# A new order for all engines, and two halves of the last output block kept apart, in a fused attention and state-space kernel

## The chip, the cores and the metric

The kernel runs on one core of a Trainium2 chip. Its engines are TensorE (PE, matmuls, which write PSUM), VectorE (DVE), ScalarE (ACT), GpSimd (POOL) and the queue of SyncE (SP), from which nearly all transfers are issued. PSUM has eight banks, each of which holds one 128 x 512 float32 tile. The metric is the device time of one execution in microseconds (us). Each engine works through its own instructions in the order in which the program gives them, and semaphores make it wait for the others.

## The reference

Two blocks without a common input, their outputs side by side, for 2048 tokens of width 448:

```python
# A: sliding, dilated attention; 16 heads of 28; 8 keys at distances 0, 2, .. 14
qkv = x @ wqkv                        # (2048, 1344)
logits[h, s, w] = q[h, s] . k[h, s - 2 * w] * 28 ** -0.5   # masked where s - 2w < 0
a = (softmax(logits) . v, heads joined) @ wo
# B: a diagonal state-space layer with a complex state of 448
Bu = x @ B_bar.T
h[t] = Lam_bar * h[t - 1] + Bu[t]
y = 2 * Re(h @ C.T) + x * Dskip
out = concatenate([a, y], -1)         # (1, 2048, 896) bfloat16
```

## The kernel before

The program is a set of small steps and one long text, `ORDER`, that names 559 of them in the order in which they are emitted. A step such as `QK021@67` is the function `QK` with the digits as arguments, and `@67` names the PSUM banks that it takes. A dot behind an eviction means that ACT does it, an equals sign DVE. Every engine, and the SP queue, gets its own steps in the order of that text, so the text sets all orders at once. A step that takes a bank waits until the step that evicts the bank's last tile is done.

The steps that matter here, with their lines:

- Set-up (L139 to L222, ahead of `ORDER`): loads of x and of the weights on SP, and `wq6`, a packed copy of the last 64 columns of q and k, which POOL makes (L222) when those columns have landed.
- `XI`, `XA`, `XH`: transposes of x on PE; `xi`, `xa`, `xh` evict them into `xT`. `WV4` is four matmuls on zeros that nothing reads.
- `QK u m k` (L332, matmuls at L242): the projections q and k for half u of the tokens and column block m, into two banks. With k = 0 it is three matmuls of 128 rows for each of two token halves s; with k = 1 the last 64 rows, the two halves side by side in the array. Whichever of the two comes first starts the sum. Column block m = 6 takes its weights from `wq6`. `QS` is the same for one s alone. `qk u m s` and `qh u s a` evict. `V_` and `v` do the same for v.
- `P u r ws` (L367): DVE multiplies q with four shifted copies of k, 128 x 2048; 28 of them. `E_ u r` (L379) sums them over the head with PE. `lt`, `TR`, `tr` turn the logits; `sma`, `smb`, `smc` are the softmax of one half u on DVE, ACT, DVE.
- `AL g`, `al`, `ad g`, `sp g` (L448 to L475): the weights of four token tiles are put into a band: PE shifts them, `al` evicts them into `Ak`, `ad` writes that to DRAM (`pd`), and the four transfers of `sp` read it back skewed into four slots of `PT`, which `pm` (POOL, L842) has zeroed. `PT` has 12 slots for 16 tiles, so `sp3` writes the slots of `sp0` again, and must wait until the AV steps of B = 0 have read them. `pm0`, `pm1`, `pm2` zero the slots of `sp0`, `sp1`, `sp2`; `pm3` zeroes `wo`, `pm4` the last two `Ak`. `OP` opens these late buffers in the place of the early ones, among them `Cn`, which the transposes `CD` read.
- `AV B hg par` (L495): attention output of half B; B = 0 needs `sp0` and `sp1`, B = 1 needs `sp2` and `sp3`. `av` evicts, `W_ b par` (L516) multiplies with `wo`, `w` evicts into one of six `ya` buffers, `ow` stores it.
- `LC`, `ci`, `CD`, `ca`, `cs`: the weights C, loaded, put together, transposed by DMA into `Cw`, and scaled.
- `BU g jp k`, `BR`, `z` (L680 to L697): B block, state group g, the inputs of four neighbouring tokens and their rotation; `UP`, `y` go up one level, `sa`, `sb`, `sd` scan pairs of groups on DVE, `DN`, `dn`, `H_`, `h` go back down.
- `C j ct`, `c`, `oc` (L774 to L789): the output block for token j of four and token tile ct: seven matmuls, an addition of x * Dskip (`xd` makes it) into one of eight buffers in `xnA`, a store. The block (2, 3) is done as two halves of 224 columns, `CH i`, `ch i`, `oh i`.

Of the kernel before, what the change touches and what calls it, by code (L numbers as in the profile page):

```python
# [11 lines left out]
ALU = mybir.AluOpType  # L12
ACTF = mybir.ActivationFunctionType

S, D, H, DH, W = 2048, 448, 16, 28, 8
# [6 lines left out]
HS = 4  # L22
# [7 lines left out]


ORDER = """
WU@0 XI0@1567 XI1 PP@2 xi0= xi1. xi2= xi3. WV4 QS00@3 pcopy pa pb QS10@4 qk000. pd_ pc XH1@5 pe XA10@6 xh1. XA11@7 ty0 xa10=
QK021@01 ty5 QK031@23 qk010. xa11= QS11@5 tf0 pf QS01@6 tf5 QK041@74 P000 QK020 qk001. ts05 ts00 pg QK040 ts15 ts10
ts20 qk021. QK030 qk041. rb2 ts25 qk011. QK050@61 qk030. P001 qk040. QK051 qk020. rb3 V_011@45 QK061@27 qk031. V_010
ty1 P010 ty2 qk051. QK060 qk050. tf1 v010. P011 V_100@03 ts01 v011. qh011. P020 V_001@16 V_101 V_111@45 V_000 v101.
P021 ts11 ts21 V_110 qh001. tf2 v100. qh000. P030 QK100@30 v000. hc0 qh010. rb0 QK110@21 v111. v001. ty4 E_00@7
v110. tf4 E_01@5 ts02 E_02 ts12 P031 ts04 QK101 QK111 V_401@64 V_400 qk111. P040 qk110. ts22 QK130@12 qk101= qk100.
v401. P041 BD v400. QK131 ts14 QK141@30 P050 QK161@46 ts24 QK140 ty3 qk130. P051 qk131. QK160 ty6 P060 E_03 qh100.
tf3 E_04 qk140. E_05 xt3 qk141. P061 V_500@12 qh101. qh110. tf6 qh111. E_06 ts03 V_501 P100 QK151@30 xt0 ts13  # L40
QK121@46 hc1 QK150 lt00 P101 v501. lt01 QK120 P110 ts06 xt1 v500. P111 TR0@7 qk120. E_10@2 qk150. V_511@14 P120
tr0. V_510 xt2 qk121. P121 V_410@37 qk151. ts16 v511. sma0 E_11@5 ts23 E_12 v510. V_411 v411. P130 v410. LC BU401@60
ts26 BU201@41 smb0 BU301@73 P131 BU300 P140 BU200 OZ z30. P141 XR BU400 z20. P150 BR31 BR21 z40. BU000@74 P151 z31.
ci0. P160 E_13 ci3. E_14 CD0 E_15 P161 ci2. BU001 BU311@63 BU310 z21. smc0 CD3 z00. ci1. BR41 BR32 CD2 E_16 z32.
BU210@17 lt10 lt11 CD1 z41. TR1@6 rb1 BU500@25 tr1. BR33 sma1 BR01 BU101@06 z33. z01. BU211 BU501 BU100 z50. xd1 OP
pm3 smb1 BR22 pm0 UP3 wo BU010@42 z22. smc1 z10. y3. BU011 ca3 BU111@10 AL0@3 BR02 BR11 al0. BR51 BU110 z11. ad0 pm1
z02. xd2 z51. BR12 AL1@3 z12. BR23 BR03 al1= ca6 BU601@64 BU511@51 xd3 BR13 ad1 BU510 z03. sp0 cs3 z13. z23. pm4 cs6
UP1 BR52 UP0 y1. UP2 xd0 BU600 y0. ca1 sa0 sp1 AL2@3 pm2 BU410@02 z52. z60. y2. sb0 ca4 BR61 BU411 BU611@56 BR42 sd0
BR53 BU610 al2. z61. ad2 z42. BR62 cs1 z53. DN0@7 DN1@3 z62. AL3@4 dn0 UP5 dn1 BR43 al3. H_20@0 sa2 BR63 z43. H_10@5
ad3 H_11@7 z63. UP4 y5. H_01@3 UP6 y4. H_21@4 sp2 H_00@1 y6. AV030@2 h10 ca2 AV010@6 h20 AV011@5 h11 av030. AV031@0  # L50
cs4 av010. AV000@7 av031. h01 AV020@2 av000. sb2 AV021@6 av020. AV001@0 av011. W_10@3 h21 ca5 sp3 sd2 W_30@7 av021.
W_20@2 av001. sa4 W_00@5 w20. DN2@4 DN3@6 ow20 w00. W_21@0 w30. ow00 dn2 W_11@2 w10. dn3 ow30 w21. sb4 W_31@5 ow10
ow21 H_13@7 H_22@4 w31. h00 H_02@3 H_23@6 ow31 H_03@0 w11. cs2 W_01@5 h02 ow11 ca0 H_12@1 AV131@2 h23 cs5 AV130@3
w01. sd4 AV101@6 av130. ow01 AV111@5 av131. AV100@3 av101. sa6 av111. AV121@2 av100. AV110@6 av121. h13 AV120@5
av110= DN4@3 W_71@2 av120. sb6 DN5@7 dn4 W_61@6 w71. sd6 W_41@5 ow71 w61. dn5 W_40@3 h03 w41. W_70@2 ow41 w40= ow61
h22 H_05@6 H_24@7 w70. ow40 W_60@5 h12 ow70 h24 DN6@0 H_15@3 W_51@4 cs0 W_50@2 h15 w51. w60. dn6 H_14@1 ow51 C32@7
w50= ow60 h14 H_04@4 C33@3 c32 h05 h04 H_26@0 H_25@5 c33 H_16@2 C31@1 h16 oc33 h26 oc32 C30@7 c31 oc31 C12@6 c30 h25
oc30 C10@4 c12 oc12 H_06@3 C21@2 h06 c10 C00@0 c21 oc10 oc21 C13@1 c00 oc00 C20@7 ow50 C02@5 C22@6 C01@3 c22 c20
oc22 c13 C11@4 oc20 c02 oc13 oc02 C03@2 c11 c01 oc11 CH0@0 oc01 c03 CH1@6 ch0 oc03 oh0 ch1 oh1
"""  # L60

@with_exitstack
def kernel(
# [17 lines left out]
    V = nc.vector  # L81
# [3 lines left out]
    SP = nc.sync  # L85
# [26 lines left out]
    def evict(e, o, i):  # L112
        (ACT.copy if e == "A" else V.tensor_copy)(o, i)  # L113
# [5 lines left out]
    xnA = xbuf.rearrange("p (t d) -> p t d", d=D)  # L119
# [39 lines left out]
    xnB = keep.tile([128, 4, T, D], BF16, tag="xnB")  # L159
# [65 lines left out]
    Ak0 = smp.tile([128, 2, 2560], BF16, tag="Ak0")  # L225
    V.memset(Ak0.rearrange("p k n -> p (k n)").bitcast(F32), 0.0)
    pds = [dram.tile([128, 2560], BF16, tag=f"pd{g}", name=f"pd{g}") for g in range(4)]
# [5 lines left out]
    pp = {}  # L233
# [214 lines left out]
    def AL(g):  # L448
# [5 lines left out]
        for w in range(W):  # L454
            cc = 32 * (3 - w // 2) + 16 * (w % 2)
            PE.matmul(p4[:, :, :, w, :], shf[:, 135 + w:263 + w], at(4 * g, 4, cc), start=(w == 0), stop=True, skip_group_check=True)  # L456
            if w > 0:
                n = 4 if g < 3 else 2
                PE.matmul(p4[:, 0:n, :, w, :], shf[:, 7 + w:135 + w], at(4 * g + 2, n, cc), start=False, stop=True,
                          skip_group_check=True)  # L460

    @op
    def al(g, e):
        evict(e, late["Ak"][g].rearrange("p (s n) -> p s n", n=40 * HS)[:, :, 0:W * HS],
              pp.pop(("al", g)).rearrange("p (s n) -> p s n", n=W * HS))

    @op
    def ad(g):
        SP.dma_start(pds[g][:], late["Ak"][g])

    @op
    def sp(g):
# [298 lines left out]
    out_b = out[0].rearrange("(q p h j) n -> j h q p n", q=2, p=128, h=2)  # L771
# [30 lines left out]
    @op  # L802
    def ch(i):
        j, ct = LAST
        if i == 0:
            pp["yo"] = xnA[:, late["m"] % 8]
            late["m"] += 1
        sl = slice(D // 2 * i, D // 2 * (i + 1))
        V.tensor_tensor(pp["yo"][:, sl], pp.pop(("ch", i))[:, 0:D // 2], xnB[:, ct, j, sl], ALU.add)

    @op
    def oh(i):
        j, ct = LAST
        SP.dma_start(out_b[j, ct // 2, ct % 2, :, D + D // 2 * i:D + D // 2 * (i + 1)], pp["yo"][:, D // 2 * i:D // 2 * (i + 1)])


    late = {}
# [39 lines left out]
    for step in ORDER.split():  # L857
        name, args, bank, e = re.fullmatch(r"([A-Za-z]+_?)(\d*)@?(\d*)([.=]?)", step).groups()
# [33 lines left out]
```

## Time and profile before

| | us |
|---|---|
| median of 3 runs | 135.94 (135.54 to 136.13) |
| the profiled execution | 135.48 |
| its span on the core | 133.3 |
| PE busy | 126.3 |
| DVE busy | 113.0 |
| ACT busy | 92.0 |
| POOL busy | 19.7 |

The span runs from the first to the last instruction of the program; the execution has 2.2 us more around it. A PE that is busy in the profile has a matmul in the pipeline; the time from one start to the next tells how long the array is taken. In the timeline and the chain of waits the columns are the start in us, the length in us, the engine, the line, what is written and read, and the count; in brackets stands how long the engine was idle before, and what ended that.

### The profile page before, as it was taken

The page shows a single profiled execution, that of the slowest core. Times are in us where ns is not written, and L with a number is a line of the kernel's source. Part 1 is how long each engine was busy: PE and PEld are TensorE (multiplying, and loading weights), DVE is VectorE, ACT ScalarE, POOL GpSimd, SP SyncE. Part 2 cuts the span into 40 slices and gives each one's busy share as a digit, 9 for nine tenths or more (in the row PEclk, how much of TensorE's full clock was granted, in tenths as well). Part 3 has the DMA queues.
Part 4 walks back from the last instruction along what each step waited for, and adds up shares of the span by engine and source line. Part 5 has one row for each costly group of instructions (what it writes and reads, how often), then busy time and mean ns, then how long its engine had stood idle before and what let it go on. Part 6 is the DMA issues. An engine that isn't in the chain of part 4 may idle for free.

```text
span 133.3 us, 2883 instructions
## 1 busy us (share of the span) xinstructions
PE 126.3 (95%) x1075; PEld 63.8 (48%) x1085; DVE 113.0 (85%) x204; ACT 92.0 (69%) x187; POOL 19.7 (15%) x37
## 2 busy tenths in 40 slices
PE   6999999999999989999999999999599999999990
PEld 6642434443334424334444536954395555555560
DVE  5579999959999999998898999999989999560581
ACT  3369999999899989987999999996496320000000
POOL 6701000000000000111999700000000000000000
PEclk9999999999999999999999999999999999999999
DMA  3886999899999987998107999699520422222052
GB/s 110 217 211 147 311 281 178 179 195 266 226 145 221 210 216 208 389 174 183 35 16 307 220 169 291 228 190 181 183 70 30 144 72 67 73 82 90 17 185 73
DMA packets 45348, 22.62 MB, mean 170 GB/s; under 512 B 33239, under 2 KB 44311, under 8 KB 45335
## 3 DMA queue, kind: packets, MB, share of 16 engines
q1 hardware_dynamic: 45272, 22.45, 72.2%
q8 instruction: 8, 0.13, 0.5%
q14 instruction: 5, 0.04, 0.1%
q10 hardware_dynamic: 63, 0.01, 0.0%
HBM read 11.68 MB, written 6.29 MB: 135 GB/s over the span
## 4 chain that ended last, share of the span: by engine, by line
PE 89%; DMA 4%; ACT 3%; issue 1%; DVE 0%; ACTq 0%
PE ps L242 39%; PE ps L779 15%; PE ps L506 6%; PE ps L519 5%; PE ps L388 4%; DMA out_dram<-ya 4%; PE ps L694 3%; PE ps L760 2%; PE ps L345 2%; PE ps L260 2%; PE ps L284 1%; PE ps L799 1%; PE ps L346 1%; PE ps L392 1%; PE ps L456 1%
## 5 line engine op out<-in xcount | busy, mean ns | idle before, releaser
L376 DVE TENSOR_TENSOR pr<-qf,kf 128x2048 bf16<-128x2048 bf16 x24 | 28.0, 1217 | 0.0
L242 PE MATMUL ps<-xbuf,BT 128*128 128x512 bf16 (+1 forms) x109 | 24.0, 379 | 0.8 <-issue 0.5
L242 PE MATMUL ps<-xT,wq 128*128 128x512 bf16 (+1 forms) x92 | 20.2, 379 | 0.3 <-issue 0.2
L779 PE MATMUL ps<-Cw,Z 128*128 128x448 bf16 x105 | 20.5, 352 | 0.0
L113 ACT CAST Z<-ps 128x512 bf16<-128x512 f32 (+1 forms) x35 | 15.5, 513 | 1.8 <-PE ps L694 0.8
L242 PEld LDWEIGHTS <-BT 128*128 128x128 bf16 (+1 forms) x112 | 8.8, 97 | 12.9 <-issue 4.5
L779 PEld LDWEIGHTS <-Z 128*128 128x128 bf16 x105 | 10.3, 98 | 9.7
L785 DVE TENSOR_TENSOR xbuf<-ps,xnB 128x448 bf16<-128x448 f32 x15 | 9.0, 620 | 7.0 <-PE ps L779 6.7
L765 DVE TENSOR_TENSOR Z<-ps,Z 128x512 bf16<-128x512 f32 x21 | 13.7, 678 | 0.9 <-PE ps L760 0.9
L519 PE MATMUL ps<-wo,oT 128*128 128x448 bf16 x64 | 13.2, 352 | 0.0
L242 PEld LDWEIGHTS <-wq 128*128 128x128 bf16 (+1 forms) x96 | 7.7, 97 | 10.9 <-issue 2.5
L242 PE MATMUL ps<-wq,xT 128*128 128x448 bf16 (+1 forms) x64 | 12.4, 354 | 0.0
L113 ACT CAST ya<-ps 128x448 bf16<-128x448 f32 (+1 forms) x15 | 7.6, 542 | 6.9 <-PE ps L519 4.5
L849 POOL MEMSET PT<- 128x4320 f32 x3 | 11.0, 3699 | 5.6 <-ACT attn L113 5.6
L656 ACT ACTIVATE ctmp<-Cw,c2t 64x448 f32<-64x448 bf16 x14 | 9.3, 667 | 0.3
L519 PEld LDWEIGHTS <-oT 128*128 128x128 bf16 x64 | 6.2, 98 | 5.7 <-ACT oT L113 0.2
L113 ACT CAST v_s<-ps 128x448 bf16<-128x448 f32 x16 | 8.5, 552 | 0.5 <-PE ps L242 0.5
L506 PE MATMUL ps<-PT,v_s 128*32 128x135 bf16 (+1 forms) x256 | 8.6, 299 | 0.0
L242 PEld LDWEIGHTS <-xT 128*128 128x128 bf16 (+1 forms) x64 | 5.0, 97 | 7.2 <-issue 3.5
L113 ACT CAST oT<-ps 128x512 bf16<-128x512 f32 x16 | 8.2, 611 | 0.1
L506 PEld LDWEIGHTS <-v_s 128*32 128x32 bf16 x256 | 7.0, 110 | 0.6 <-ACT Z L113 0.4
L113 ACT CAST kf<-ps 128x512 bf16<-128x512 f32 x12 | 6.8, 604 | 0.0
(153 smaller groups left out, 186.8 us busy)
## 6 DMA issues: line engine op xcount, KB each, us to landing
PT<-pd SPq DMA_DIRECT2D x16, 156.0 KB, 5.3
xnB<-in_B_x_dram SPq DMA_DIRECT2D x2, 896.0 KB
out_dram<-ya SPq DMA_DIRECT2D x16, 112.0 KB, 2.5
out_dram<-xbuf SPq DMA_DIRECT2D x15, 112.0 KB, 1.7
pd<-Ak SPq DMA_DIRECT2D x2, 640.0 KB, 2.9
xbuf<-in_A_x_dram SPq DMA_DIRECT2D x2, 448.0 KB
xnB<-in_B_x_dram SPq DMA_DIRECT2D x4, 224.0 KB, 5.8
xnB<-in_B_x_dram SPq DMA_DIRECT2D x4, 192.0 KB, 4.7
```

Of the source, the lines that this page charges most:

```text
L113: (ACT.copy if e == "A" else V.tensor_copy)(o, i)
L242: PE.matmul(o, l, r, start=(first and i == 0), stop=(not first and i == len(pairs) - 1 and not more[s]))
L376: V.tensor_tensor(t[:], q.unsqueeze(1).to_broadcast((128, 4, 512)), k4, ALU.mult)
L388: PE.matmul(acc[s][32 * i:32 * i + 32], E[:, f, ws, :], t[:, i, :], start=(f == 0 and ws == 0), stop=False)
L506: PE.matmul(p[32 * hh:32 * hh + 32, 128 * bl:128 * bl + n], v_s[:, t, 4 * hg + hh, :], PT[:, t % NS, (4 * hg + hh) // HS, (4 * hg + hh) % ...
L519: PE.matmul(p[:, 0:D], late["oT"][:, b // 4, hg, par, 128 * (b % 4):128 * (b % 4) + 128], late["wo"][:, hg, :], start=(hg == 0), stop=(hg ...
L656: ACT.activation(t[a:a + 64, 0:D], Cw[b:b + 64, g, :], ACTF.Copy, scale=c2t[a:a + 64, g:g + 1])
L694: PE.matmul(pp["z", g, j][:], rot(g, 0), late["Z"][:, g, j - 1, :], start=False, stop=True)
L765: V.tensor_tensor(zz, pp.pop(("h", j, g))[:], zz, ALU.add)
L779: PE.matmul(p[:, 0:D], z, Cw[:, g, :], start=(g == 0), stop=(g == G - 1))
L785: V.tensor_tensor(yo, pp.pop(("c", j, ct))[:, 0:D], xnB[:, ct, j, :], ALU.add)
L849: POOL.memset(late["PT"][:, 4 * i:4 * i + 4].rearrange("p t g n -> p (t g n)").bitcast(F32), 0.0)
```

## The change

`ORDER` is replaced as a whole: the same 559 steps, in another order, with other banks, and with 24 evictions on the other engine (19 from ACT to DVE, 5 from DVE to ACT). Some of its lines, of the start, of the middle, and of the end (`WU@0` to `oh1` before, `WU@0` to `oh0` after):

```diff
-WU@0 XI0@1567 XI1 PP@2 xi0= xi1. xi2= xi3. WV4 QS00@3 pcopy pa pb QS10@4 qk000. pd_ pc XH1@5 pe XA10@6 xh1. XA11@7 ty0 xa10=
-QK021@01 ty5 QK031@23 qk010. xa11= QS11@5 tf0 pf QS01@6 tf5 QK041@74 P000 QK020 qk001. ts05 ts00 pg QK040 ts15 ts10
...
-UP1 BR52 UP0 y1. UP2 xd0 BU600 y0. ca1 sa0 sp1 AL2@3 pm2 BU410@02 z52. z60. y2. sb0 ca4 BR61 BU411 BU611@56 BR42 sd0
...
-ad3 H_11@7 z63. UP4 y5. H_01@3 UP6 y4. H_21@4 sp2 H_00@1 y6. AV030@2 h10 ca2 AV010@6 h20 AV011@5 h11 av030. AV031@0
...
-oc22 c13 C11@4 oc20 c02 oc13 oc02 C03@2 c11 c01 oc11 CH0@0 oc01 c03 CH1@6 ch0 oc03 oh0 ch1 oh1
+WU@0 XI0@1234 XI1 xi1= PP@5 xi0. xi2. pcopy pa xi3= QS00@6 pb pc pe QS10@7 qk000. qk010. XH1@1 XA10@2 xh1. pd_ ty2
+XA11@5 xa10= WV4 QK061@34 tf2 xa11= ty0 tf0 QK021@67 QK031@10 QK030 qk030= pf pg qk031. ts00 QK060 P000 qh011. QK020
...
+qk100. P060 E_05 E_06 lt00 QK121@30 v110. rb0 P110 P100 QK161@21 QK120 qk120. ts16 QK160 P111 V_511@47 qh100. qk121.
+ty4 QK151@53 qh101. V_510 v511. P121 P101 P130 QK150 E_11@0 tf4 E_10@2 v510. lt01 qh111. qk151. P131 TR0@7 V_500@46
+qk150. ts04 ts26 qh110. P120 ts14 xt0 V_410@35 hc1 V_411 tr0. v410. V_501 v500. LC E_12 E_13 XR P141 OZ P140 E_14
+BU401@17 v501. P150 P160 ts24 BU301@34 BU300 z30. P151 BU400 P161 ci1. BR31 z31. z40. sma0 smb0 E_15 E_16 lt10 ci0=
+BU311@63 BU201@41 BU310 lt11 ci3= v411. BR32 BU200 z20. BU210@20 BR21 z21. z32. ci2= CD2 BR41 TR1@5 BU000@41 z41. smc0
+CD0 xd0 tr1. sma1 BR33 z33= AL0@6 al0. CD1 BU001 BU211 z00. BU101@75 BU100 xd3 smb1 BR01 CD3 OP pm3 BU500@64 z10= z01.
+BR22 z22. smc1 BR11 z11. BU010@17 BU011 BU501 ca3 BU111@25 ad0 rb2 BR23 z23= BR02 z02. BU110 BR12 BR03 AL1@1 UP2 z50.
+BR51 z03. wo al1. pm4 y2. z12= AL2@6 al2. BR13 UP0 AL3@2 BU601@10 z51= pm0 al3. BU511@46 z13= UP1 y0= BU600 ca1 cs3
+BU510 BR52 y1= BU410@72 ca2 sp0 z60. UP3 pm2 z52. pm1 y3. BR53 sa0 ad1 sb0 BU611@51 BU411 z53. sd0 BR42 cs1 BR61 UP5
+z61. DN0@4 y5. BU610 BR62 z42. cs2 ca6 z62. sa2 sb2 BR43 ad2 sp1 AV020@3 AV031@0 AV030@6 av020. ad3 AV011@7 av011. sp2
+AV010@5 av010. AV021@3 av031. AV001@7 av001. AV000@5 av021. DN1@0 BR63 z43. W_31@7 rb1 W_11@3 sd2 dn1 sp3 av030. DN2@6
...
+W_21@7 h22 w21. W_30@4 w30. h12 ow31 sb4 ow21 sd4 AV111@1 AV120@7 AV121@2 av121= ca0 AV110@0 AV101@4 av111. av101.
...
+w00. cs4 H_00@4 h00 cs5 DN6@6 w40= w70. w10. H_24@3 W_61@0 ow71 H_15@7 H_23@5 w50= C33@4 h23 c33 H_20@2 dn6 C30@1
...
+C00@1 oc21 oc30 CH1@5 h10 h14 C11@6 ch1 c11 oh1 C13@3 C02@2 c13 C03@7 oc13 oc11 c00 c02 oc02 oc00 c22 c03 oc03 C12@5
+w61. ow61 C10@0 c12 oc12 oc22 c10 oc10 C01@6 c01 oc01 CH0@3 ch0 oh0
```

The functions:

```diff
+    def ak(g):
+        return Ak0[:, g] if g < 2 else late["Ak"][g]
+
     @op
     def al(g, e):
-        evict(e, late["Ak"][g].rearrange("p (s n) -> p s n", n=40 * HS)[:, :, 0:W * HS],
+        evict(e, ak(g).rearrange("p (s n) -> p s n", n=40 * HS)[:, :, 0:W * HS],
               pp.pop(("al", g)).rearrange("p (s n) -> p s n", n=W * HS))
 
     @op
     def ad(g):
-        SP.dma_start(pds[g][:], late["Ak"][g])
+        SP.dma_start(pds[g][:], ak(g))
...
     def ch(i):
         j, ct = LAST
-        if i == 0:
-            pp["yo"] = xnA[:, late["m"] % 8]
-            late["m"] += 1
+        yo = pp["yo", "half", i] = xnA[:, late["m"] % 8]
+        late["m"] += 1
         sl = slice(D // 2 * i, D // 2 * (i + 1))
-        V.tensor_tensor(pp["yo"][:, sl], pp.pop(("ch", i))[:, 0:D // 2], xnB[:, ct, j, sl], ALU.add)
+        V.tensor_tensor(yo[:, sl], pp.pop(("ch", i))[:, 0:D // 2], xnB[:, ct, j, sl], ALU.add)
```

`oh(i)` stores from the buffer of its own half. `ak` gives the first two bands their place before `OP` has run, so that `al0` may stand ahead of it. In the SP queue the new order has `CD2 CD0 CD1 CD3 ad0 wo sp0 ad1 ad2 sp1 ad3 sp2 sp3`, where the old one has `CD0 CD3 CD2 CD1 wo ad0 ad1 sp0 sp1 ad2 ad3 sp2 sp3`; on POOL `pm3 pm4 pm0 pm2 pm1` for `pm3 pm0 pm1 pm4 pm2`.

More of the change, by code (lines that the diff above doesn't have):

```diff
@@ L32 @@
 ORDER = """
-WU@0 XI0@1567 XI1 PP@2 xi0= xi1. xi2= xi3. WV4 QS00@3 pcopy pa pb QS10@4 qk000. pd_ pc XH1@5 pe XA10@6 xh1. XA11@7 ty0 xa10=
-QK021@01 ty5 QK031@23 qk010. xa11= QS11@5 tf0 pf QS01@6 tf5 QK041@74 P000 QK020 qk001. ts05 ts00 pg QK040 ts15 ts10
-ts20 qk021. QK030 qk041. rb2 ts25 qk011. QK050@61 qk030. P001 qk040. QK051 qk020. rb3 V_011@45 QK061@27 qk031. V_010
-ty1 P010 ty2 qk051. QK060 qk050. tf1 v010. P011 V_100@03 ts01 v011. qh011. P020 V_001@16 V_101 V_111@45 V_000 v101.
-P021 ts11 ts21 V_110 qh001. tf2 v100. qh000. P030 QK100@30 v000. hc0 qh010. rb0 QK110@21 v111. v001. ty4 E_00@7
@@ L38 @@
[L38 to L47, printed above, removed]
@@ L48 @@
-UP1 BR52 UP0 y1. UP2 xd0 BU600 y0. ca1 sa0 sp1 AL2@3 pm2 BU410@02 z52. z60. y2. sb0 ca4 BR61 BU411 BU611@56 BR42 sd0
-BR53 BU610 al2. z61. ad2 z42. BR62 cs1 z53. DN0@7 DN1@3 z62. AL3@4 dn0 UP5 dn1 BR43 al3. H_20@0 sa2 BR63 z43. H_10@5
-ad3 H_11@7 z63. UP4 y5. H_01@3 UP6 y4. H_21@4 sp2 H_00@1 y6. AV030@2 h10 ca2 AV010@6 h20 AV011@5 h11 av030. AV031@0
-cs4 av010. AV000@7 av031. h01 AV020@2 av000. sb2 AV021@6 av020. AV001@0 av011. W_10@3 h21 ca5 sp3 sd2 W_30@7 av021.
-W_20@2 av001. sa4 W_00@5 w20. DN2@4 DN3@6 ow20 w00. W_21@0 w30. ow00 dn2 W_11@2 w10. dn3 ow30 w21. sb4 W_31@5 ow10
@@ L53 @@
[L53 to L57, printed above, removed]
@@ L58 @@
-oc30 C10@4 c12 oc12 H_06@3 C21@2 h06 c10 C00@0 c21 oc10 oc21 C13@1 c00 oc00 C20@7 ow50 C02@5 C22@6 C01@3 c22 c20
-oc22 c13 C11@4 oc20 c02 oc13 oc02 C03@2 c11 c01 oc11 CH0@0 oc01 c03 CH1@6 ch0 oc03 oh0 ch1 oh1
+WU@0 XI0@1234 XI1 xi1= PP@5 xi0. xi2. pcopy pa xi3= QS00@6 pb pc pe QS10@7 qk000. qk010. XH1@1 XA10@2 xh1. pd_ ty2
+XA11@5 xa10= WV4 QK061@34 tf2 xa11= ty0 tf0 QK021@67 QK031@10 QK030 qk030= pf pg qk031. ts00 QK060 P000 qh011. QK020
+qk021. qh010. P030 BD QK050@25 P031 QS11@1 qk020. P020 P001 ts02 ts12 QK041@07 qk011. qh000. QK051 ts22 qk050.
@@ new lines @@
+V_011@46 xt3 QK040 V_010 xt1 ty5 qk040. ts10 QS01@1 qk041. V_001@20 qk051. E_00@7 qk001. v011. P021 E_02 tf5 qh001.
+P010 V_000 xt2 ts20 P011 ts05 v010. ts15 ts25 V_100@51 E_01@6 ty3 E_03 v000= V_401@34 v001. tf3 rb3 V_101 ty1 tf1
+v100. hc0 ts03 ts13 V_400 P061 QK130@20 QK131 v400. V_111@53 qk130. v401. qk131. P051 V_110 QK110@24 v101. P040 QK111
+ts01 ts23 P041 ty6 tf6 qk111. QK141@01 QK140 qk110. P050 v111. ts11 QK100@42 ts21 ts06 qk140. QK101 qk101. E_04 qk141.
+qk100. P060 E_05 E_06 lt00 QK121@30 v110. rb0 P110 P100 QK161@21 QK120 qk120. ts16 QK160 P111 V_511@47 qh100. qk121.
@@ new lines @@
+w31= cs6 DN3@0 dn3 UP4 dn2 z63. W_01@7 y4. sa4 w11. UP6 dn0 H_13@2 H_21@0 H_12@3 y6= av000. h13 H_22@6 h21 w01. W_10@5
+W_21@7 h22 w21. W_30@4 w30. h12 ow31 sb4 ow21 sd4 AV111@1 AV120@7 AV121@2 av121= ca0 AV110@0 AV101@4 av111. av101.
+av120. AV100@6 AV131@3 av100. cs0 av131. sa6 AV130@1 av110. av130. W_20@4 H_03@7 DN4@6 w20= W_51@3 w51. sb6 ow11
+W_60@2 dn4 W_00@0 ow30 W_50@1 ow51 h03 sd6 H_02@3 DN5@4 dn5 ow01 h02 W_71@6 ca4 ow20 w60. ca5 W_70@7 W_40@2 ow60 w71.
+w00. cs4 H_00@4 h00 cs5 DN6@6 w40= w70. w10. H_24@3 W_61@0 ow71 H_15@7 H_23@5 w50= C33@4 h23 c33 H_20@2 dn6 C30@1
@@ L60 @@
+H_26@5 H_06@4 h24 H_25@6 ow70 h15 H_16@3 h06 xd2 h20 oc33 h25 C31@7 h26 C32@4 C21@2 ow10 H_04@6 c32 ow50 H_01@5 c30
+h16 xd1 H_05@4 h05 ow00 c21 c31 C20@1 oc32 ow40 oc31 c20 oc20 W_41@3 w41. ow41 h01 C22@4 h04 H_10@2 H_11@3 h11 H_14@7
+C00@1 oc21 oc30 CH1@5 h10 h14 C11@6 ch1 c11 oh1 C13@3 C02@2 c13 C03@7 oc13 oc11 c00 c02 oc02 oc00 c22 c03 oc03 C12@5
+w61. ow61 C10@0 c12 oc12 oc22 c10 oc10 C01@6 c01 oc01 CH0@3 ch0 oh0
 """
@@ L813, in oh @@
         j, ct = LAST
-        SP.dma_start(out_b[j, ct // 2, ct % 2, :, D + D // 2 * i:D + D // 2 * (i + 1)], pp["yo"][:, D // 2 * i:D // 2 * (i + 1)])
+        SP.dma_start(out_b[j, ct // 2, ct % 2, :, D + D // 2 * i:D + D // 2 * (i + 1)], pp.pop(("yo", "half", i))[:, D // 2 * i:D // 2 * (i + 1)])
     late = {}
```

## The prediction

> **What bounds the kernel now.** I read the page first.
>
> ```profile
> span 133.3 us, 2883 instructions
> PE 126.3 (95%) x1075; PEld 63.8 (48%) x1085; DVE 113.0 (85%) x204; ACT 92.0 (69%) x187; POOL 19.7 (15%) x37
> PE   6999999999999989999999999999599999999990
> DVE  5579999959999999998898999999989999560581
> ```
>
> TensorE (PE) is full from slice 1 to 38, with one hole in slice 30. VectorE (DVE) is full too, but only up to slice 33: PE sets the end, and DVE has its room in the last quarter. Next, the chain of waits in order of time: what PE's work costs back to back, and what the holes are.
>
> ```profile
> 7.41 0.32 PE ps L346
> 16.50 9.66 PE ps L242 x51
> 28.32 1.41 PE ps L388 x24
> 48.30 0.32 ACT v_s L113
> 82.54 4.09 PE ps L506 x113
> 89.91 4.91 DMA out_dram<-ya
> 95.18 0.54 ACT ya L113
> 100.66 0.89 PE ps L519 x4
> 116.74 0.22 PE ps L760
> 116.96 11.92 PE ps L779 x63
> ```
>
> One 512-column matmul starts every 0.216 us (six in 1.29 us elsewhere in this view), a half-row one where the row layout changes takes 0.32, so a change of layout costs 0.1; a step E_ is 0.43, an AV 0.51, a W_ 0.76, a C 1.32, an H_ 0.22. Adding the steps of the old order so, with its 47 changes of layout, gives 124.7 us; with the start at 1.05 PE would end at 125.8. It ends at 130.2. I call this sum "bare" (up to any step, in an engine's own order, without a wait) and what the clock shows above it "lag"; on DVE and ACT each step counts with the busy time that it adds in the trace, DVE from 4.2 us on, after its set-up work. PE's lag in the trace is 0.5 at 10 us, 1.3 at 47, 2.0 at 50 (v411 on ScalarE, ACT, held a PSUM bank), 2.2 at the first AV, 4.1 at 101 (hole at 94.3: w11 had no free ya buffer until an output landed at 94.8) and 4.4 at the end. So about 3 us are waits that an order can win. Behind PE come 3.1 us (last addition, transfer, end), and 2.2 us of the execution lie outside the span: 135.48 against 133.3. The median is 0.46 above that execution.
>
> **What the change removes, adds and moves.** The same 559 steps stay: 120.04 us of matmuls on PE in both orders, with 50 changes of layout for 47: +0.3, so a bare end at 126.1. Net 14 evictions go from ACT to DVE, at 0.6 to 0.7 us for 512 columns (qf 683 ns on DVE against 595 on ACT) and 0.4 for 256; DVE's own bare sum goes from 114.4 to 121.2, ACT's falls by about 7. The split of the last block gives each half its own buffer and moves CH1 ahead: the last step stays one half, its addition (392 ns) and its transfer, so the tail costs what it did: 0 (the wait that could be gone, ch1 behind ch0, is 0). ak() lets the first al and ad stand ahead of the opening of the late buffers: issues only, 0. What counts is therefore where PE's lag changes. No term below is under 0: the old order's waits are not in the bare sum, so a wait that does not come is 0.
>
> The start. QK061 needs wq6, which GpSimd (POOL) copies, and the new order puts it first among the half-row projections; the old one had it at 18.3 us. The timeline:
>
> ```profile
> 9.07 0.84 PE L302 MATMUL ps<-ident,xbuf 128*128 128x128 bf16 x12
> 9.18 0.58 ACT L113 COPY xT<-ps 64x512 bf16<-64x512 bf16 x1 [0.33 <-PE ps L316]
> 9.85 0.61 PE L242 MATMUL ps<-xT,wq 64*128 64x512 bf16 x4
> 10.83 0.65 POOL L222 COPY wq<-wq 128x512 bf16<-128x512 bf16 x1 [4.46 <-DMA wq<-in_A_wqkv_dram]
> ```
>
> The loads ahead of that copy are set-up code and do not move, so wq6 is there at 11.48. PE stands at QK061 by 9.8 (bare 9.3 and 0.5), and QK021, QK031 and QK030 are queued behind it. It starts at 11.55: +1.8 of lag (1.6 to 2.0). Only WV4, 0.25 us of idle matmuls, covers some of it, inside that count. Further drift to 48 us, without the bank waits: +0.3 (0 to 0.7, the old order's own).
>
> DVE inherits it: qk030= waits for the first half of QK030 (11.55 + three pairs of 0.22 and a change + five matmuls and 0.38 for the last: 13.6), ends at 14.3 where its bare sum is 10.6, lag 3.7, and pg, P000 and all products stand behind it. The products are 24 of 28:
>
> ```profile
> L376 DVE TENSOR_TENSOR pr<-qf,kf 128x2048 bf16<-128x2048 bf16 x24 | 28.0, 1217 | 0.0
> ```
>
> that is 1.14 each once overlapped, with no idle to give lag back. P121 then needs qk121, on ACT behind qh100, which needs QK160's first tile: bare 39.3 + 2.6 = 41.9, two evictions 0.56 and 0.5: 42.9. DVE comes at 37.4 + 3.9 = 41.3 and waits 1.6: lag 5.5. E_14 needs P140: 46.0 + 5.5 = 51.5. PE would be there at 47.6 + 2.6 = 50.2: +1.3 (0 to 1.6). The E_ steps after it agree within 0.3.
>
> Mid part. smb0, lt10 and lt11 wait on ACT for sma0 (52.4 + 5.5), so the banks of BU210 come free at 60.2 instead of 59.7, and z10= on DVE holds BR11 by 0.2: +0.5 (0 to 0.9). PE's lag is now 4.4.
>
> The band transfers, from SP's timeline, and then POOL's:
>
> ```profile
> 59.41 1.25 SPq L649 DMA_TRANSPOSE Cw<-Cn  x1
> 69.08 2.80 SPq L469 DMA_DIRECT2D pd<-Ak  x2
> 72.12 5.68 SPq L475 DMA_DIRECT2D PT<-pd  x8
> 84.42 4.91 SPq L475 DMA_DIRECT2D PT<-pd  x8
> ```
>
> ```profile
> 62.71 7.34 POOL L849 MEMSET PT<- 128x4320 f32 x2 [5.62 <-ACT attn L113]
> ```
>
> Old order: AL1 ends at 70.4, the last sp1 is issued at 76.9, the first AV runs at 82.5: 12.1 us from AL1 to AV, all covered. The new order has 9.8 us of PE work there. AL1 ends at 68.9 + 4.4 = 73.3, al1 (behind z50 and z03) at 74.1; ad1 lands 2.9 us after issue (row pd<-Ak), 77.1; sp1's four issues run to 79.2, and such a transfer lands 4.0 to 5.9 us after issue: with 5.0 at 84.2. PE comes at 78.7 + 4.4 = 83.1: +1.1. Ends: 0.1 with 4.0; 4.5 with 5.9 and ad1 at 5.4, the row of pd<-oT, since ad2 is now close behind; 2.9 is nearest because ad1 starts alone. POOL's path to sp1 is nearly as late: ci2= on DVE ends at 59.6, CD2, CD0 and CD1 take 1.3 each on SP, CD1 lands 3.3 later at 65.4, then pm0, pm2, pm1 at 3.70: 76.5.
>
> Behind AV. W_31 waits for av001 and av021 on ACT: +0.4 (0 to 0.6). sp3 may only start when AV000 has read PT (82.7 + 5.5, and 0.2): its four issues and 5.0 end at 94.9, PE is at AV111 at 89.1 + 5.9 = 95.0; with 5.9 it waits 0.8: +0.3 (0 to 1.2). In the last part DVE follows PE at once (h01, h04 in front of C00, c30 in front of C20): +0.3 (0 to 1.0).
>
> Sum of lags: 0.5 + 1.8 + 0.3 + 1.3 + 0.5 + 1.1 + 0.4 + 0.3 + 0.3 = 6.5, for 4.4 before. PE ends at 126.1 + 6.5 = 132.6, the span is 135.7, the execution 137.9, and 138.3 on the scale of the median.
>
> [...] The row: the 27 warm-up matmuls start 104 ns apart over 2.9 us, later ones of that shape 56 apart; after the 1.44 us hole at 94.3 the PEclk row stays at 9, so I add nothing to my waits. [...]
>
> **The rivals.** One: faster. The transfers and products arrive in time, and only the wait at QK061 stays: lag 0.5 + 1.8 + 0.7 + 0.2, end 129.3, execution 134.6, median scale 135.0; with a shorter drift 134.6. It speaks for it that no ya buffer and no v411 is waited for any more (2.4 us of old lag gone), against it the 9.8 us between AL1 and AV. It decides whether the last sp1 lands by 82. Chance 0.17.
>
> Two: no change. E_14 and the AV wait shrink to half (1.2 together), the small ones to 0.8: lag 4.3, and 136.1. Chance 0.08.
>
> Three: slower still, DVE becoming the bound to the end. Its bare sum 121.2 and a lag of 9.5 instead of 8.5 make PE wait for each h ahead of C30, C21 and C00: each us of that lag is about a us, 139.3 and more. Against it, DVE has 4 us of room behind the last h. Chance 0.12.
>
> Four: the AV wait at its upper end, 4.5 (+3.4), and PE slow after it as at the start, where 2.9 us at double distance cost 1.4: 143.1. Against it, ad1 starts alone. Chance 0.03.
>
> **How the numbers follow.** The forecast has 0.60. The range goes from 134.8, inside the faster rival, to 140.6, above the third; some 0.12 lie below and 0.08 above (the fourth, and the upper ends of the terms). A measurement tells about 0.5% (0.7 us) from no change: slower 0.75, same 0.08, faster 0.17.
>
> **What would show it.** Right: an idle PE ahead of L242 from about 10.0 to 11.5, ended by POOL; a first P (L376) near 16.5 instead of 12.6; a DVE wait for ACT near 42; a PE wait ahead of L506 in slice 24 or 25, ended by DMA PT<-pd; no wait for ya. Wrong: first AV before 82 us, or PE's last start before 130.

## The result, and the profile after

The changed kernel takes 137.0 us (median of 6 executions, 136.83 to 138.79); the kernel before took 136.05 beside it (135.54 to 137.95). The ratio is 1.0114, with a 95% interval of 1.0074 to 1.0153: slower by about 1.1% (by the two medians 0.7%). Medians are over all executions of a kernel; ratios leave out the slow ones, more than 1.5% above the fastest of the same kernel. The forecast was 138.3, in a range of 134.8 to 140.6. The profiled execution took 137.08; one execution, the 138.79, has a mean granted clock of 0.988, which the last section takes up.

First the page of the changed kernel: the span, the busy times, the rows of PE and DVE over 40 slices, and the shares of the chain that ended last.

```profile
span 135.0 us, 2884 instructions
...
PE 127.2 (94%) x1085; PEld 63.6 (47%) x1085; DVE 118.9 (88%) x218; ACT 86.3 (64%) x173; POOL 19.8 (15%) x37
...
PE   6995999999999998979999999999999999999990
...
DVE  5476799989999999979899999999999999995751
...
PE 59%; DVE 23%; ACT 6%; SPq 5%; issue 2%; DMA 2%; POOL 1%; ACTq 0%
```

The span grew from 133.3 to 135.0. Counted from 0, PE has no hole in slice 28 any more (the forecast calls it slice 30); it has one in slice 3 instead, and smaller ones in slices 15 and 17. DVE is full up to slice 35, where it was full up to 33. The waits of PE, longest first (us in total, times, longest):

```profile
PE ps L242 <- POOL wq L222: 1.6, 1, 1.6
PE ps L260 <- DVE wz L116: 1.1, 1, 1.1
PE ps L242 <- ACT lt L399: 0.8, 1, 0.8
PE ps L388 <- DVE pr L376: 0.7, 1, 0.7
PE ps L345 <- ACT xT L113: 0.2, 1, 0.2
```

The second line is the start, the same in both kernels. The others come to 3.3 us, and the two that the old order had behind it (v411, and the 1.44 us for `ya`) are gone. The chain of waits (start, length, what) shows the first one: loads issued one behind another on SP, ten of them weight loads, then the transfer of the last, POOL's copy, and then PE.

```profile
8.61 2.47 DMA wq<-in_A_wqkv_dram
...
11.13 0.70 POOL wq L222
...
11.88 4.16 PE ps L242 x21
```

The same view from 48 us on shows the other two. DVE's products end at 51.1 for E_14, and run on to 55.7; then sma0, then ACT with smb0 and, behind it, lt10 and lt11, for whose banks PE stands at BU210 until 61.1. Of ACT's part 1.28 us is a table load that comes with the exponential of smb0.

```profile
51.06 4.63 DVE pr L376 x4
...
57.74 1.28 ACT L427
...
59.03 1.06 ACT attn L427
60.09 0.98 ACT lt L399 x2
...
61.11 1.24 PE ps L242 x5
```

And no wait of PE for `PT`: in SP's timeline sp1 is issued from 77.7 on,

```profile
74.68 0.35 SPq L472 DMA_DIRECT2D pd<-Ak  x1
75.50 0.34 SPq L472 DMA_DIRECT2D pd<-oT  x1
77.71 1.97 SPq L478 DMA_DIRECT2D PT<-pd  x4
```

its last transfer lands at 83.47, and PE comes to the first AV at 83.65 from other work, 0.2 us later.

### The profile page after: what moved, and what is told of

It reads as the page before. It is cut to its first block, busy times and chain, and to the rows that moved or that the text cites. A ratio compares the mean times of both kernels' runs of the same rounds, so it can differ in the third digit from the quotient of the medians.

```text
span 135.0 us, 2884 instructions
## 1 busy us (share of the span) xinstructions
PE 127.2 (94%) x1085; PEld 63.6 (47%) x1085; DVE 118.9 (88%) x218; ACT 86.3 (64%) x173; POOL 19.8 (15%) x37
## 4 chain that ended last, share of the span: by engine, by line
PE 59%; DVE 23%; ACT 6%; SPq 5%; issue 2%; DMA 2%; POOL 1%; ACTq 0%
PE ps L242 30%; PE ps L782 13%; DVE pr L376 6%; DVE Z L768 4%; PE ps L697 3%; PE ps L509 3%; SPq L131 2%; PE ps L388 2%; SPq L137 2%; DMA wq<-in_A_wqkv_dram 2%; DVE ya L113 2%; PE ps L763 2%; DVE Cw L663 2%; DVE Z L756 2%; DVE hs L738 1%
## 5 line engine op out<-in xcount | busy, mean ns | idle before, releaser
L782 PE MATMUL ps<-Cw,Z 128*128 128x448 bf16 x105 | 21.2, 353 | 0.1
L113 ACT CAST Z<-ps 128x512 bf16<-128x512 f32 (+1 forms) x26 | 12.7, 527 | 6.0 <-PE ps L697 3.2
L113 ACT CAST ya<-ps 128x448 bf16<-128x448 f32 (+1 forms) x13 | 6.6, 544 | 14.3 <-PE ps L522 14.1
L242 PE MATMUL ps<-wq,xT 128*128 128x448 bf16 (+1 forms) x64 | 12.9, 354 | 0.0
L509 PE MATMUL ps<-PT,v_s 128*32 128x135 bf16 (+1 forms) x256 | 8.4, 300 | 0.0
L113 ACT CAST v_s<-ps 128x448 bf16<-128x448 f32 x15 | 7.7, 537 | 0.0
L113 ACT CAST qf<-ps 128x512 bf16<-128x512 f32 x12 | 6.7, 581 | 1.4 <-PE ps L242 1.4
L509 PEld LDWEIGHTS <-v_s 128*32 128x32 bf16 x256 | 7.2, 112 | 0.4 <-issue 0.4
```

Source lines behind the costliest of these rows:

```text
L242: PE.matmul(o, l, r, start=(first and i == 0), stop=(not first and i == len(pairs) - 1 and not more[s]))
L509: PE.matmul(p[32 * hh:32 * hh + 32, 128 * bl:128 * bl + n], v_s[:, t, 4 * hg + hh, :], PT[:, t % NS, (4 * hg + hh) // HS, (4 * hg + hh) % ...
L782: PE.matmul(p[:, 0:D], z, Cw[:, g, :], start=(g == 0), stop=(g == G - 1))
```

## The experiments

Theory A: the loss is made by waits that the new order sets up early: the one for `wq6`, and then two on what DVE passes on because its first products start 4.3 us later (16.91 against 12.59): E_14 and, with ACT's order, BU210. Rival B: the loss is the 14 evictions that DVE got. Rival C: the band transfers at AV cost what the forecast gave them. All kernels below ran beside the kernel before, and the ratio is to that kernel; "lag" is meant as in the prediction.

| kernel | median us | ratio | 95% interval |
|---|---|---|---|
| the change | 137.0 | 1.0114 | 1.0074 to 1.0153 |
| wq6_late | 136.07 | 1.0026 | 0.999 to 1.0061 |
| lt_first | 136.83 | 1.0076 | 1.0052 to 1.0099 |
| qk030_act | 136.3 | 1.0047 | 1.0017 to 1.0078 |
| three_mends | 135.13 | 0.9996 | 0.9951 to 1.0042 |
| p000_early | 134.85 | 0.9936 | 0.9913 to 0.996 |
| before_wq6_wait | 138.25 | 1.0121 | 1.0068 to 1.0174 |
| wait_filled | 137.0 | 1.0114 | 1.0068 to 1.0159 |
| before_halves | 135.53 | 0.9995 | 0.9973 to 1.0017 |
| sp1_behind_ad3 | 139.05 | 1.0252 | 1.0225 to 1.0279 |
| late_on_act | 139.46 | 1.0301 | 1.0251 to 1.0351 |
| early_and_act | 137.39 | 1.0126 | 1.0087 to 1.0165 |
| warm_up_40 | 137.29 | 1.0117 | 1.0076 to 1.0158 |

**wq6_late**: the changed kernel, with the step that needs `wq6` some 2 us further back.

```diff
-WV4 QK061@34 tf2
+WV4 tf2
...
-ts00 QK060 P000
+ts00 QK061@34 QK060 P000
```

> The changed order, with QK061 moved from the front of the half-row projections to just ahead of QK060 (two changes of row layout more, +0.2 us). Theory A (PE's 1.6 us wait for wq6 starts the loss, and DVE's product chain hands it on): the wait at 10.3 us is gone, qk030= starts at 12.5 instead of 13.9 and the first product near 15.6 instead of 16.9, the wait at E_14 stays between 0.5 and 1.0, and the time falls by 1.0 to 1.6, to 135.4 to 136.0. Theory B (the 14 evictions moved to DVE make the loss, the wait at the start is hidden behind DVE): under 0.4, 136.6 to 137.2. Theory C (the band transfers would hold PE at the first AV, where the last sp1 landed only 0.2 us ahead): the wait comes back ahead of L509, time 136.5 to 137.

Measured 136.07, just above the 135.4 to 136.0 expected; profiled 135.8, which is 1.3 below the profiled execution of the change. Its waits of PE:

```profile
PE ps L260 <- DVE wz L116: 1.1, 1, 1.1
PE ps L242 <- ACT lt L399: 0.8, 1, 0.8
PE ps L388 <- DVE pr L376: 0.8, 1, 0.8
PE ps L509 <- issue: 0.3, 1, 0.3
```

The wait for POOL is gone and nothing of its size is in its place; the two later ones stay. So the wait for `wq6` is most of the loss, and those two do not come from it: DVE's first product came 1.26 us earlier (15.65 for 16.91), but PE came to E_14 earlier by as much, and waits there as long as before.

**lt_first**: lt10 and lt11 ahead of smb0 on ACT.

```diff
-sma0 smb0 E_15 E_16 lt10 ci0=
-BU311@63 BU201@41 BU310 lt11 ci3=
+sma0 E_15 E_16 lt10 lt11 smb0 ci0=
+BU311@63 BU201@41 BU310 ci3=
```

> The changed order, with lt10 and lt11 ahead of smb0 on ACT, which stood idle from 56.4 to 57.7. Theory A (BU210's wait for two PSUM banks is a wait of its own, worth up to 0.9): the 0.8 us gap at 59.8 is gone; AL0, which needs smc0, then waits some 0.3, and the time falls by 0.4 to 0.8, to 136.2 to 136.6. Rival (the gap only comes back at AL0 or at the first AV, as both hang on smb0): under 0.2, 136.8 to 137.1.

```profile
PE ps L242 <- POOL wq L222: 1.6, 1, 1.6
PE ps L260 <- DVE wz L116: 1.1, 1, 1.1
PE ps L388 <- DVE pr L376: 0.7, 1, 0.7
PE ps L456 <- DVE attn L437: 0.3, 1, 0.3
```

The 0.8 us at BU210 is gone; 0.3 comes back at AL0, which waits for the end of the softmax (L437) that smb0 is part of. The time falls by 0.2 us by the medians and by 0.4% by the ratios, whose intervals overlap: the hole had ACT's order as its cause, but what it was worth is not clear of the noise, and is less than its length.

**qk030_act**: the eviction qk030, on which the first DVE product stands, on ACT and behind pg.

```diff
-QK030 qk030= pf pg qk031.
+QK030 pf pg qk030. qk031.
```

> The changed order, with the one early eviction qk030 back on ACT, behind pf, so that DVE does not stand for QK030. Theory A (DVE's lag hands the early wait on to E_14 and BU210): the wait for wq6 stays at 1.6, DVE's first product starts 1.5 to 2 us sooner, the gap at E_14 (0.74) goes and that at BU210 (0.9) shrinks to under 0.3: time down by 1.2 to 1.8, 135.2 to 135.8. Rival (PE alone sets the end after the wait for wq6, and the gaps at E_14 and BU210 belong to ACT): the gaps stay, under 0.4, 136.6 to 137.2.

Measured 136.3, 0.7 below the change, where 1.2 to 1.8 was expected.

```profile
PE ps L242 <- ACT lt L399: 0.8, 1, 0.8
PE ps L388 <- DVE pr L376: 0.2, 1, 0.2
```

PE's wait ahead of L388 (E_14) falls from 0.7 to 0.2, the one ahead of BU210 stays at 0.8. The first half says that E_14's wait is DVE's start, handed on; the second, that BU210 is not: DVE's part there came earlier, and ACT's table load and exponential still stood ahead of lt10. The eviction qk030 is one of the 19 that the change moved to DVE, so this much of rival B holds.

**three_mends**: the three edits together. 

> The changed order with all three edits of the first runs: QK061 ahead of QK060, lt10 and lt11 ahead of smb0, qk030 on ACT. Theory A (the three waits are links of one lag, each mended where it arises): no gap at 10.3, E_14 under 0.6, BU210 none, AL0 under 0.3; PE's last matmul ends 2.0 to 2.6 us sooner than in the changed order, time 134.4 to 135.0, below the old order by 0.5 to 1.0. Rival (the first AV and the band transfers hold PE as soon as it comes earlier): a wait ahead of L509 of 0.5 to 1.5, time 135.2 to 136.

Measured 135.13: by the ratio level with the old order. Five of the nine executions took 134.74 to 135.13, the other four 136.53 to 136.8; the profiled one is of the four, with PE's first projections at 1.44 us for three matmuls, where p000_early has 0.86 (last section). Its waits of PE behind the start are these two:

```profile
PE ps L388 <- DVE pr L376: 0.4, 1, 0.4
PE ps L456 <- DVE attn L437: 0.3, 1, 0.3
```

The rival's wait ahead of L509 is not there. The changed kernel's loss is these three waits: with them it goes.

**p000_early**: three_mends, and DVE begins its first product ahead of pg, the second behind it.

```diff
-tf0 QK021@67 QK031@10 QK030 pf pg qk030.
+tf0 P000 QK021@67 QK031@10 QK030 pf pg qk030.
...
-QK061@34 QK060 P000 qh011.
+QK061@34 QK060 P001 qh011.
...
-P020 P001 ts02
+P020 ts02
```

> As the kernel with the three edits, and on DVE P000 ahead of pg and P001 behind it, so that DVE multiplies while pf on ACT is not done. Theory A: the first product starts at 12.5 instead of some 15.5, no gap at E_14, time 133.8 to 134.5. Rival (DVE's lag no longer counts once QK030's eviction is off it): as the kernel with the three edits, within 0.2.

Measured 134.85, ratio 0.9936 (0.9913 to 0.996): below both kernels, though above the 133.8 to 134.5 expected. From the page of the profiled execution, 134.33:

```profile
span 132.1 us, 2885 instructions
...
PE   6999999999999999999999999999999999999990
```

and all of PE's waits over 0.2 us:

```profile
PE ps L260 <- DVE wz L116: 1.1, 1, 1.1
PE ps L388 <- DVE pr L376: 0.3, 1, 0.3
PE ps L345 <- ACT xT L113: 0.2, 1, 0.2
```

P000 runs at 12.16 instead of 16.91; DVE had been idle there. With its three waits out and this product in, the new order is 0.9 us better than the old one (134.85 for 135.78 in the same runs). What the product adds to three_mends is not shown: the two intervals overlap, and the lower five executions of three_mends lie in the same range.

**before_wq6_wait**: the old order with one matmul that reads `wq6`, put ahead of QK021. 

> The old order with one more matmul of 128 columns on zeros (0.06 us) ahead of QK021, whose weights are wq6, so that PE must wait for POOL's copy there as the changed order does; nothing else is moved. Theory A: PE waits 1.6 us at 10 us, and the time rises by 1.0 to 1.8, to 137.0 to 137.8: the wait alone is as large as the whole loss of the change. Rival (the old order's later waits, v411 at 48 and the ya buffer at 94, swallow it): 136.0 to 136.6.

PE idles 1.62 us there, from 10.34 to 11.96, and the holes at v411 (0.19, as before) and for `ya` (1.0, it was 1.44) are still there. The ratio, 1.0121, is that of the whole change: this one wait is enough to lose what the change lost, and the old holes later in the order hide little of it. Four of the eight executions, at a granted clock of 1.0, took 137.28 to 137.67, as expected; the other four, at 0.974 to 0.988, took 138.82 to 140.39.

**wait_filled**: the same, with 24 matmuls on zeros (six more `WV4`) in the idle time. 

> The old order with the same early need of wq6 as in the experiment before_wq6_wait, but with 24 matmuls on zeros in front of it, so that PE idles some 0.25 us there instead of 1.6. Theory W (PE's clock is set in turns of 3.41 us, and a turn in which PE was idle for more than some 1.61 us is followed by one at half rate): no execution has a half-rate turn behind the wait, so the median falls from 138.25 to 137.3 to 137.6, the cost of the wait itself (1.6) staying, and no execution is above 138.3. Rival (the half rate has another cause than the idle time, or comes at random): the spread stays, 137.3 to 140.4 with a median near 138.2.

Measured 137.0, ratio 1.0114, a little below the 137.3 to 137.6 expected. Theory W rests on the profiled executions of the last section: clock 0.50 for 3.41 us behind a window of 3.41 us in which PE was idle for 1.67 (before_wq6_wait), and full rate behind one with 1.61 idle (the change). It was right on the spread: the six executions have a granted clock of 0.998 to 1.0, where four of eight had 0.974 to 0.988 in before_wq6_wait. The cost, some 1.5 us (135.55 for the kernel before in these runs), stays, though PE now works on zeros where it waited.

**before_halves**: the old order with the new `ch` and `oh`, each half in its own buffer. 

> The old order with the two halves of the last block in buffers of their own, nothing else. Theory A (the halves give nothing: no wait of ch1 or oh1 on the other half was in the trace): within 0.2 of the old kernel, ratio 0.998 to 1.002. Rival (oh0 and ch1 shared a tile, so that ch1 or the store waited): 0.3 to 0.5 faster.

Ratio 0.9995 (0.9973 to 1.0017): the split of the last block is worth nothing that can be measured, as the forecast had it.

**sp1_behind_ad3**: the changed kernel, ad3 ahead of sp1 on SP.

```diff
-BR43 ad2 sp1 AV020@3 AV031@0 AV030@6 av020. ad3 AV011@7
+BR43 ad2 ad3 sp1 AV020@3 AV031@0 AV030@6 av020. AV011@7
```

> The changed order with ad3 (640 KB) issued ahead of sp1 on SP. Theory A (the first AV's wait of 1.1 us was not seen only because sp1 lands 4.2 us after its issue, 0.2 us ahead of PE): sp1 starts 0.4 to 0.6 later and shares the engines with ad3, so a gap of 0.3 to 1.5 opens ahead of L509 at 83.6, time up by 0.2 to 1.2. Rival (PE has room there): no gap, time within 0.2.

Measured 139.05, 2.05 above the change, more than the 0.2 to 1.2 expected. The wait of the forecast is there now, and is 1.6 of it; the rest is not accounted for:

```profile
PE ps L509 <- DMA PT<-pd: 1.6, 1, 1.6
```

with sp1's issues running from 78.03 to 81.1 (in the change 77.7 to 79.7), and the two transfers of this stretch whose landing is recorded landing 5.0 and 5.5 us after issue. So the mechanism of rival C is real, and in the change it is covered by no more than the 0.2 us seen above. One transfer in front of it uncovers it.

**late_on_act**: the changed kernel with eight evictions back on ACT, each an edit of one sign, `z33=` to `z33.` and so on.

> The changed kernel with eight of the evictions that moved to DVE (z33, z10, z23, z12, z51, z13, y0, y1) on ACT again. Theory A (the loss is made by the waits up to BU210; behind it DVE's lag of 8 us reaches PE by 0.4 only): 136.6 to 137.1, a gain of at most 0.4. Rival B (the 14 evictions that DVE got are the loss): DVE is some 5 us less busy, and the time falls to 135.6 to 136.2.

Both expectations fell, on the same side: 139.46, slower than the change by 2.5 us. One wait of DVE and three of PE are new:

```profile
DVE p L723 <- ACT Z L113: 6.0, 1, 6.0
...
PE ps L750 <- DVE Z L745: 0.9, 1, 0.9
...
PE ps L697 <- ACT Z L113: 0.7, 1, 0.7
...
PE ps L709 <- ACT Z L113: 0.5, 1, 0.5
```

The evictions between 64 and 79 us (z33 to y1) stand on ACT behind al, ca and each other, and ACT is busy for 13.3 of these 15 us; DVE's first scan (L723) then waits 6.0 us for them, PE 1.2 for what they write, and DN0 0.9 for the scan. DVE is 3.3 us less busy (115.6 for 118.9) and the kernel slower: these evictions on DVE are what the new order does well. Rival B falls for these eight; of the other moved evictions only qk030 was tried by itself.

**early_and_act**: the same on top of p000_early. 

> p000_early with the same eight evictions on ACT. Theory A: 134.6 to 135.0, no difference from p000_early (134.85) that can be measured. Rival B: 134.0 or less. A version that beats both kernels is looked for here too.

137.39, again 2.5 us above its base. The same loss on both bases shows that it has nothing to do with the early waits.

**warm_up_40**: p000_early with 40 warm-up matmuls for 27, to see whether the executions still differ by a late full rate as the profiled ones of three_mends and p000_early do (from 10.51 us on and from 3.95; last section). 

> p000_early with 40 warm-up matmuls on zeros instead of 27. [...]

The executions lie within 0.3 us of each other (136.99 to 137.3), but five executions don't prove much, and the price is 2.4 us. An estimate from the spacing in the trace before, 56 to 106 ns from start to start, gives 0.7 to 1.4 us for the 13 matmuls. In the timeline 1.2 of it is a stop of PE in the middle that p000_early does not have:

```profile
86.42 0.79 PE L522 MATMUL ps<-wo,oT 128*128 128x448 bf16 x3
88.43 0.74 PE L522 MATMUL ps<-wo,oT 128*128 128x448 bf16 x3 [1.23 <-issue]
```

"issue" means that PE waited for nothing that the profile shows. One of the eight 16 KB transfers of instructions lies ahead of it, from 85.46 to 86.87, beside the band transfers (the DMA queues from 85 to 89 us: packets, MB, share of the 16 engines):

```profile
q8 instruction: 1, 0.02, 2.2%
```

p000_early has such a transfer there too (84.31 to 85.69), without a stop, so the transfer is not shown to be the cause. Whether the 26 added instructions moved it to a worse place was not tried; this stays open.

## Why the prediction was right, and which of its terms were not

The sign, the first cause and the interval were right; 1.3 us of the 138.3 were not there. Of these, 0.8 are PE's: its last matmul ends at 131.8, where 132.6 was forecast. The other 0.5 is the step to the median: 0.46 was added for it, and here the median lies 0.08 below the profiled execution. By the terms of the sum, with lag read from the trace in the same way:

| term | forecast | trace after |
|---|---|---|
| start | 0.5 | 0.9 at 9.8 us |
| QK061 waits for wq6 | 1.8 | 1.7 |
| drift to 48 us | 0.3 | 0 |
| E_14 | 1.3 | 1.1, 0.74 of it idle |
| BU210 | 0.5 | 1.1, 0.92 of it idle |
| AV020 waits for sp1 | 1.1 | 0 |
| W_31, AV111 | 0.4 + 0.3 | 0 |
| late part | 0.3 | 0.9 |
| sum | 6.5 | 5.7 |

The sum after is 131.8 less the bare 126.1, and the late part is what the rows above it leave.

**QK061.** The forecast start was 11.55, the trace has 11.88, because POOL's last load landed 0.3 later; PE came 0.4 later too. wq6_late and before_wq6_wait show it from both sides: 0.9% of time is gained back without it (1.0114 to 1.0026), and 1.2% is lost when it alone is put into the old order.

**DVE's start and E_14.** The first product was forecast near 16.5 and ran at 16.91, with a DVE lag of 4.2 at the end of qk030= (forecast 3.7) and 4.55 at P000. The wait of P121 for qk121, 1.6 in the forecast, did not come, and could not: I misread what the step needs. r = 2 is the first half of the tokens, for which qk120 is evicted; qk121 is read first by P130, which starts at 44.60, 1.6 us after qk121 has ended. DVE's lag went up in another way, by 0.7 between 24 and 35 us, most of it at tf3, whose second instruction waits 0.51 for ACT (at 28.2), and stood at 5.4 at P121, for 5.5 in the forecast. So E_14 came out near its forecast by luck: two errors cancelled. qk030_act shows the part that stands: with the 0.7 of qk030 out of DVE's start, 0.5 of E_14's wait goes.

**BU210** was under-sized, 0.5 for 1.1. PE came near the forecast (59.8 for 59.7) and so did the end of sma0 on DVE (57.7 for 57.9), but the forecast let the banks come free 2.3 after that. The trace has 3.4, all of it on ACT: the table load of 1.28, 1.06 of exponential, and lt10 and lt11 behind them with 0.98. The forecast left about one of these out, and lt_first takes the wait away by ACT's order alone.

**AV020** is the term that failed. Its two ends were 0.1 and 4.5, and I took a landing of 5.0 us after sp1's last issue; it took 4.3 (79.20 to 83.47). The landings recorded:

```profile
DMA to landing us min/median/max: 3.5/4.2/5.5
```

(the view of the tile `PT`, for the five of its 16 transfers whose landing is recorded; before it was 4.0/5.3/5.9, for four). The row that I took came from a stretch where sp0 and sp1 went out as eight transfers in one go; here sp1 goes out as four, after ad2. That the number in one go makes the difference is not shown. The fourth issue came at 79.2, as forecast, and with 5.0 the wait would have been 0.6; the other half of the 1.1 went because PE came 0.55 later than forecast (83.65 for 83.1), BU210 having cost more. For sp3 I had used 5.0 too; the one of its four whose landing is recorded took 3.5, and AV111 did not wait. W_31's 0.4 did not come either: ACT had av001 and av021 done in time.

**The tail, the halves, ak()** were put at nothing, and before_halves bears out the halves. **Two readings** are off without weight: the hole for `ya` lies in slice 28, not 30, and the warm-up matmuls start 106 ns apart, not 104.

**The rivals**: the third, DVE the bound to the end, did not come: DVE's lag is 8.0 late in the kernel, under the 9.5 that it needed. It was near, though. The chain that ended last runs over DVE without a break for 20 us:

```profile
89.10 0.62 DVE ya L113
...
109.44 0.34 DVE Z L756
109.83 0.36 PE ps L782
```

PE loses little in that stretch, in pieces of 0.25 us at most by the starts of its steps; its lag goes from 4.8 at BU210 to 5.7 at the end. Of the first, faster, the mechanism was right as far as it went (no late transfer, nothing for `ya`), but E_14 and BU210 waited too: the one for DVE, which stood for qk030 (qk030_act), the other for ACT's order (lt_first). Neither was handed on from QK061, for both stay in wq6_late. The fourth did not come; that PE is slow after a wait of 4.5 us, its term of 1.4, no run shows, for PE has no wait that long in any. What the runs have in its place is clock 0.50 for 3.41 us behind the wait of 1.62 in before_wq6_wait.

## What to carry to other kernels

Before a new order is costed, look for the first step of each engine that needs a result from the slow set-up (a late load, a copy on POOL): a step moved ahead of that costs most of its wait, here 0.9 to 1.3 us of time for 1.6 of wait. Where a step waits for a bank, ask which engine's order holds the bank, not only which engine was late; and do not count on the whole length of a wait that is taken out, for some of it comes back further on (0.3 of the 0.8 in lt_first). An eviction is not better on the engine that is less busy over the whole span: the eight that went back to ACT cost 2.5 us, because ACT was full in that stretch (13.3 of 15 us).

## What the runs showed of the hardware that was not expected

**Half rate after a wait of 1.62 us.** The forecast added nothing to its waits for a slower PE. In the profiled execution of the change that is so; in that of before_wq6_wait it is not. Its view by windows of 3.41 us (length, busy time of PE, PEld, DVE, ACT, POOL, then PEclk):

```profile
8.98:12.39 3.41, 1.74 (x20) 1.18 (x21) 2.77 (x10) 3.01 (x9) 0.70 (x1) 1.00 0.79 193
12.39:15.80 3.41, 3.41 (x10) 0.67 (x7) 3.17 (x16) 1.32 (x4) 0.00 (x0) 0.50 0.94 229
15.80:19.21 3.41, 3.41 (x17) 1.29 (x16) 3.31 (x8) 2.61 (x7) 0.00 (x0) 1.00 1.10 305
```

PE was busy 1.74 of 3.41 us, and the next 3.41 went at clock 0.50. In the change, with the windows laid two times 3.41 us behind the start of full rate at 5.32, as that stretch lies behind it in before_wq6_wait (5.56 to 12.39; an estimate), PE was busy a little more, and kept its clock:

```profile
8.73:12.14 3.41, 1.80 (x25) 1.29 (x26) 2.58 (x11) 3.10 (x5) 0.69 (x1) 1.00 0.82 209
12.14:15.55 3.41, 3.41 (x20) 1.44 (x17) 1.92 (x11) 2.04 (x7) 0.00 (x0) 1.00 0.98 219
```

before_halves has the third case, at the hole for `ya`:

```profile
94.52:97.93 3.41, 1.69 (x54) 1.42 (x56) 3.33 (x8) 1.94 (x4) 0.00 (x0) 1.00 0.40 127
97.93:101.34 3.41, 3.40 (x118) 2.91 (x110) 2.50 (x7) 3.41 (x8) 0.00 (x0) 0.50 0.12 38
```

The windows of lt_first (9.69 to 13.10) and qk030_act (9.39 to 12.81) that hold the same wait, laid by the same count, were busy for 1.81 and 1.82, and the clock stayed (mean 1.0 in both). So 1.69 and 1.74 us busy were followed by clock 0.50, and 1.80, 1.81 and 1.82 were not. That is one window in each of five executions, and what sets the clock is not shown beyond them; the wait for `wq6` in the new order lies 0.06 us from the one that lost its clock. The one execution of the change at 138.79 has the mean clock 0.988 that one such stretch would give (an estimate: half of 3.41 in 136.8), and so has before_wq6_wait's at 138.82.

Where a profile has no such stretch, the place of its windows is an estimate, from the four times at which the clock was seen to fall: in before_wq6_wait at 12.39, 6.83 us or two times 3.41 after full rate began at 5.56; in before_halves at 97.93, 92.16 us or 27 times after 5.77; and behind the last instruction in the change at 135.02 and in the kernel before at 133.99, both 129.7 us or 38 times after 5.32 and 4.29. In sp1_behind_ad3 a wait as long, 1.6 us ahead of L509, lies by that count in two windows (one ends at 85.36, 22 times after 10.28), and PEclk stays at 9 in all slices.

**Full rate began at another time in these executions.** It was granted at 4.29 us in the profiled execution before, at 5.32 in that of the change, and not until 10.51 in that of three_mends. The traces have no clock record before the grant, and PEclk shows 1.00 there (in the change from 0 to 5.32); the lengths tell it. The first three projections of 512 columns, in the timeline of three_mends and then of p000_early (granted at 3.95):

```profile
6.93 1.44 PE L345 MATMUL ps<-xT,wq 128*128 128x512 bf16 x3
```

```profile
6.17 0.86 PE L345 MATMUL ps<-xT,wq 128*128 128x512 bf16 x3 [0.23 <-ACT xT L113]
```

In three_mends the transposes of `XA` began at 11.0 us instead of 8.7. An order that waits for `wq6` until 11.9 hides such a late grant: sp1_behind_ad3, granted at 10.28, shows no wait of PE for POOL at all. A new order is therefore compared by many executions and by its waits, not by one profile.
